# Attention values as plain float32 products, the two heads in the two column halves of the TensorE array

## The chip, the cores and the metric

The kernel runs on one core of a Trainium2 chip. Such a core has a matrix engine (TensorE, "PE" in the profile, with its weight loads as "PEld"), a vector engine (DVE), a scalar engine (ACT), a further vector engine that cannot reach the matrix engine's result banks (POOL), and queues that start transfers, here nearly all on SP. The matrix engine multiplies a loaded block of weights, up to 128 rows by 128 columns, with moving data of up to 512 columns, and adds into one of eight result banks, each of 128 partitions by 512 float32 values.

The metric is the device time of one launch in microseconds, the median of several runs. Lower is better.

## The reference

Eight batches of eight heads attend over 576 positions with heads of 64, masked by blocks of 64; then a feed-forward layer runs over all 4608 tokens. All inputs and the output are float32.

```python
def _attn_ref(q, k, v):                      # (8, 8, 576, 64) each
    scores = scale * np.matmul(q, k.transpose(0, 1, 3, 2))
    mask = block_i >= block_j                # blocks of 64 positions
    scores = np.where(mask, scores, -1000000000.0)
    scores = scores - np.max(scores, axis=-1, keepdims=True)
    attn = np.exp(scores)
    attn = attn / (np.sum(attn, axis=-1, keepdims=True) + 1e-09)
    return np.matmul(attn, v).astype(np.float32)

def _moe_ref(x, w_in, w_out, alpha):         # (4608, 512), (512, 2048), (2048, 512)
    h = x @ w_in
    g = np.maximum(h, 0.0) + alpha * np.minimum(h, 0.0)
    return (g @ w_out).astype(np.float32)
```

The last product of the attention, `attn @ v`, is called "the values" here.

## The kernel before

**Two ways to multiply.** A product in plain float32 is one call in the kernel. Most of the kernel does it another way: each operand is split into a high part, rounded to the type `float32r`, and a low part, the rest, and the sum of high x high, low x high and high x low is taken, each a product of the rounded type.

**Order of work.** The kernel does not issue its work as it is written. Every operation is handed to `Plan.op` with its engine, a cost, what it reads and writes, the buffers it takes, and a priority. `schedule` (L181) then plays the engines forward: whenever one is free it takes the ready operation of the lowest priority number, and the resulting order is the order of instructions in each queue. `SHIFTS` is a table that adds a small number to the priorities named in it. `Products` and the functions `c_...` give the costs that this planner counts with. `Buf` stands for a room in SBUF or a result bank that is handed out while planning. At most 6 of the 8 banks serve the attention at one time.

**Attention.** The 64 batch-heads go as 32 pairs of heads, pair `p` at priority `5 * p`. A pair has five query tiles (`query_tile`, L818): four of 128 queries of each head (j = 0 to 3) and one, j = 4, of the last 64 queries of both heads together. Each tile is scores on TensorE (L859; L854 for the early plain ones, L921 for j = 4), the maximum on DVE, the exponential on ACT (L875), the division by the sum on POOL (L883), transposes of the probabilities on TensorE (L891, L947, L956) and a copy of these out of the bank (`evac`, L961). The tiles are done in two parts: 4, 3, 2, and then 1, 0. For the first four pairs tiles 1 and 0 are done ahead of everything else.

**Values.** `values` (L976) runs after each part: for the span of queries 256 to 575 after tiles 4, 3, 2, and for 0 to 255 after tiles 1, 0. The key positions come in blocks of 128, and block c meets the queries from c * 128 on. So the later span has products of 320, 320, 320 and 192 columns and one of 64 columns for the last 64 keys, the earlier span one of 256 and one of 128. `NV = NP + 1 = 5` divides the pairs:

- Pairs 0 to 4 are plain. The transposed probabilities are copied once into `PTF` (one of two, in turn), the last block's into `P4F`. The weights are the 64 columns of V of one head, straight from where V was loaded (`vraw`). Each head's products go to partitions 0 to 63 of a bank (L994; L998 for the last 64 keys, which has 64 rows of weights), and ACT copies them to the head's half of `xT` (L1012).
- Pairs 5 to 31 are split. `evac` writes `PH` on ACT (L970) and `PL` on DVE (L971), of which there is one each. V is split into `V` on ACT and DVE (L764, L766). With the high part of the probabilities as moving data, the weights are V's high and low part side by side, 128 columns; with the low part, V's high part alone, 64 columns. For the last 64 keys both parts of the probabilities and V are stacked, `P4`. All are at L1004. The two halves of the bank are then added: ACT copies one to `tmp` (L1023) and DVE adds the other (L1025).

At pair 5 the rooms of the plain pairs (`pt0`, with `PTF` and the second room for V) are closed and those of the split pairs (`PH`, `PL`, `V`) opened.

**Feed-forward.** Chunks of 256 tokens run beside the attention for the first six of sixteen blocks of the hidden layer (`chunk_a`: L582 and L619), with low enough priorities to fill TensorE. The other ten blocks run after it, on chunks of 512 tokens (L660 and L619); their weights are prepared from about the end of the attention on (`later_weights`).

Of the kernel before, what the change touches and what calls it, by code (L numbers as in the profile page):

```python
# [9 lines left out]
F32 = mybir.dt.float32  # L10
# [10 lines left out]
NP = H // 2  # L21
NPAIR = B * NP
DM, DF, DO = H * D, 2048, 512
P = 128
# [15 lines left out]
WARM, WARM_END = 10, 3400  # L40
TICK, FULL_COLUMNS, SP0 = 3413.33, 3060, 700
LAG = 6.75
Q2B, TB = 1, 1
VP, VL, VE = 2.0, 1.0, 0.0
E0, E1 = -4.0, 1.0
NEAR, LP = 8.0, 1.0
FP = -1
XP = 2.0
AHEAD = {(8 + k // 2, k % 2): 12 + 4 * k for k in range(4)}
SHIFTS = {  # L50
    9: 2.6, 10: 1.7, 11: -0.8, 12: -0.5, 15: 2.4, 16: 2.1, 19: -5.7, 36: 3.1, 42: 1.1, 59: 0.6, 60: -0.7, 61: 1.4, 81.1574: 2.7, 99: -1,
    101.5278: -0.6, 119.5: 1.1, 121.8981: 0.2, 122.2685: 1.7, 153.5: 1.1, 154.5: 0.3, 155: -0.8, 155.5: 0.8, 156.5: -1.6, 175.2315: 1.4,
    180.4167: -1.6, 184.8611: -3.9,
}
SOON, XB = 150, 1006.7
FEW = 12
# [1 line left out]
B1 = 10  # L58
RB, EB = 2, 2
LO_A = ("POOL", "POOL")  # L60
NV = NP + 1
PB = 6
GB = 6
LAT = {"PE": 250, "DVE": 130, "ACT": 140, "POOL": 140}
# [205 lines left out]
def c_dve(n):  # L270
    return 65 + n / 0.96
# [6 lines left out]
def c_act(n, sbuf=False):  # L278
    return (93 if sbuf else 51) + n / 1.2
# [27 lines left out]
def c_mm(n, rows=P):  # L307
    return Products(max(n / 2.22, 107) + 2, max(n / 1.2, 213), n * rows / P)


def c_tr(light=False):
    return Products(109, 213, 256, 50.0, light)

# [8 lines left out]
def attn_ffn(ctx, tc, qT, kT, vT, w_in, w_out, alpha, out):  # L322
# [49 lines left out]
    def pt_key(p):  # L372
        return p % 2 if p < NV else 2

    def pt_of(p, i):

        if i == 2:
            return P4F[p % 2] if p < NV else P4
        return PTF[p % 2] if p < NV else pt[i]
# [22 lines left out]
    def rooms(pool, *kinds):  # L402
        for kind, n, shape, dt in kinds:
            plan.room(kind, n, lambda i, kind=kind, shape=shape, dt=dt: (pools[pool] if isinstance(pool, str) else pool).tile(
                [P, *shape], dt, name=f"{kind}{i}"))

    rooms(wraw, ("raw", RB, [1024], I32), ("m", EB, [512], F32))
    rooms(st, ("qraw", 1, [QP], F32), ("kraw", 1, [S], F32), ("vraw", 1, [5, 2, D], F32), ("p", PB, [512], F32), ("pl", 1, [S], F32), ("tmp", TB, [448], F32),
          ("nm", 4, [2], F32), ("nm2", 2, [2], F32), ("s", 4, [2, 2], F32), ("s3", 2, [3], F32), ("sp", 4, [2], F32), ("ri", 4, [2], F32))


# [562 lines left out]
    def values(p, v_parts, spans, pr):  # L974


        V, vkeys = v_parts
        b, pair = divmod(p, NP)
        r0 = (b * S) % RING
        shared = {q0: Buf("bank", "att") for q0, q1, _ in spans if q1 - q0 <= 256}  # L980
        for h in range(2):
            lo, hi = (slice(0, 64), slice(64, 128)) if h == 0 else (slice(64, 128), slice(0, 64))
            for q0, q1, part in spans:
                n = q1 - q0
                ob, tmp = shared.get(q0) or Buf("bank", "att"), Buf("tmp")
                at = h * n if q0 in shared else 0
                pkeys = [("PT", pt_key(p), h, j, x) for j in range(4) for x in range(2) if P * j < q1 and q0 < P * j + P]
                if q1 == S:
                    pkeys += [("PT", pt_key(p), h, j, x) for j in (4, 5) for x in range(2)]
                cs = [(c, max(q0, c * P)) for c in range(4) if c * P < q1]  # L990

                def plain(h=h, q0=q0, q1=q1, ob=ob, at=at, cs=cs):
                    for c, a in cs:
                        nc.tensor.matmul(ob()[0:64, at + a - q0:at + q1 - q0], V()[:, c, h, :],  # L994
                                         pt_of(p, 0)[:, h, 448 * c + a:448 * c + q1],
                                         start=(c == 0), stop=(c == cs[-1][0] and q1 < S))
                    if q1 == S:
                        nc.tensor.matmul(ob()[0:64, at + 512 - q0:at + S - q0], V()[0:64, 4, h, :], pt_of(p, 2)[0:64, h, :],  # L998
                                         start=False, stop=True)

                def mm(x, c, n, h=h, q0=q0, q1=q1, ob=ob, at=at, a=dict(cs)):

                    b = 512 if x == "x" else a[c]
                    nc.tensor.matmul(ob()[0:64 if x == "l" else P, at + b - q0:at + q1 - q0],  # L1004
                                     V()[:, c, 1 + h, :] if x == "l" else V()[:, c, 2 * h:2 * h + 2, :],
                                     P4[:, h, :] if x == "x" else pt[x == "l"][:, h, 448 * c + b:448 * c + q1],
                                     start=(n == 0), stop=(n < 0))
                if p < NV:
                    op("PE", sum(c_mm(4 * (q1 - a)) for _, a in cs) + (c_mm(256, 64) if q1 == S else 0), plain, r=vkeys + pkeys,
                       w=[(ob, h)], prio=pr)  # L1010
                    w = [("x", b % 2, pair, h, part)]
                    op("ACT", c_act(n), lambda ob=ob, at=at, n=n, q0=q0, hi=hi: nc.scalar.copy(  # L1012
                        out=xT[hi, pair, r0 + q0:r0 + q0 + n], in_=ob()[0:64, at:at + n]), r=[(ob, h)], w=w, prio=pr)
                    continue
                between = (("h", 1), ("h", 3), ("l", 3), ("x", 4), ("l", 0), ("l", 1), ("l", 2)) if q1 == S else (("l", 1), ("l", 0))
                for i, (x, c) in enumerate((("h", 0), *between, ("h", 2 if q1 == S else 1))):
                    last = i == len(between) + 1
                    n1 = 64 if x == "x" else q1 - dict(cs)[c]
                    op("PE", c_one(n1, x == "l"), lambda mm=mm, x=x, c=c, i=-1 if last else i: mm(x, c, i),
                       r=[*vkeys, *pkeys, *[(ob, h, "begun")] * (i > 0), *[(ob, h, k) for k in between if last], *[(ob, 0)] * (h and q0 in shared)],  # L1020
                       w=[(ob, h) if last else (ob, h, (x, c)) if i else (ob, h, "begun")], claim=[tmp] * (i == 0),
                       prio=pr + LP * (x == "l"))
                op("ACT", c_act(n) + HALF, lambda ob=ob, at=at, n=n, hi=hi, lo=lo, tmp=tmp: nc.scalar.copy(  # L1023
                    out=tmp()[hi, :n], in_=ob()[lo, at:at + n]), r=[(ob, h)], w=[tmp], prio=pr)
                op("DVE", c_dve(n) + (0 if h else HALF), lambda ob=ob, at=at, n=n, q0=q0, hi=hi, tmp=tmp: nc.vector.tensor_tensor(  # L1025
                    out=xT[hi, pair, r0 + q0:r0 + q0 + n], in0=ob()[hi, at:at + n], in1=tmp()[hi, :n], op=ALU.add),
                    r=[(ob, h), tmp], w=[("x", b % 2, pair, h, part)], prio=pr)

    def xs(b, parts=(0, 1)):
        return [("x", b % 2, pr, h, i) for pr in range(NP) for h in range(2) for i in parts]  # L1030
# [45 lines left out]
                done += CHA  # L1076

    def end_attention():
        att.close()
        pools["wb"] = ctx.enter_context(tc.tile_pool(name="wb", bufs=1, side="right"))  # L1080

# [92 lines left out]
```

## Time and profile before

| | |
|---|---|
| runs | 1126.52 us median of 3, from 1123.86 to 1128.25 |
| the profiled execution's own span | 1122.8 us |
| TensorE | 7288 products, busy 1106.1 us |
| DVE, ACT, POOL | busy 835.2, 715.3 and 613.4 us |
| values, split pairs (L1004) | 702 products, between 107.8 and 580.2 us |
| values, plain pairs (L994, L998) | 140 products, between 14.2 and 96.6 us |

Times in the views are microseconds from the start of the span, unless marked ns. In a row of a group stand the line, engine and operation, what is written and read, the shape of the weights (rows*columns) and of the moving data, the count, and then the busy time of the group and the mean duration of one in ns. Products are pipelined: the duration of one includes its way through the array, so the durations of a row of them overlap and add up to more than the time they take. What one costs is read from the pace, the time from one to the next. In the chain of waits each stretch begins where the one before it ends, so a stretch of n products there, divided by n, is the pace. The idle time of a group is followed by what ended it.

### The profile page before, as it was taken

What the parts mean: (1) busy time and instruction counts of PE and PEld (TensorE: products, weight loads), DVE (VectorE), ACT (ScalarE), POOL (GpSimd) and SP (SyncE); (2) the same over time, 40 slices, a digit from 0 to 9 for tenths busy, and PEclk for the clock granted to TensorE, in tenths of its full rate; (3) what the DMA queues carried; (4) which work ended last, traced back from release to release, by engine and by line L of the source; (5) the groups of instructions that cost most, each with busy time, mean ns of one, the idle gap of its engine ahead of it and who ended that gap; (6) DMA issues with size and microseconds to landing.
All of it is one profiled execution on the core that took longest, in us unless ns stands there. A gap on an engine that the chain in (4) does not pass through costs nothing.

```text
span 1122.8 us, 22035 instructions
## 1 busy us (share of the span) xinstructions
PE 1106.1 (99%) x7288; PEld 988.5 (88%) x7288; DVE 835.2 (74%) x1954; ACT 715.3 (64%) x1933; POOL 613.4 (55%) x769
## 2 busy tenths in 40 slices
PE   8999999999999999999999999999999999999998
PEld 5677989999999999999999888988988998998987
DVE  7888999888888888898857997564647465656554
ACT  7888988888888888788856655343434334343432
POOL 5767556656565556566549987243434334352422
PEclk9999999999999999999999999999999999999999
DMA  8797676576765576567324532221303030312021
GB/s 232 226 261 214 188 221 177 169 201 169 220 170 146 175 191 197 175 170 213 100 93 148 162 101 76 76 72 42 113 1 113 1 114 3 112 38 76 2 75 38
DMA packets 75314, 147.96 MB, mean 132 GB/s; under 512 B 9792, under 2 KB 11840, under 8 KB 75200
## 3 DMA queue, kind: packets, MB, share of 16 engines
q1 hardware_dynamic: 74768, 146.28, 44.4%
q8 instruction: 58, 0.95, 0.4%
q14 instruction: 56, 0.46, 0.1%
q10 hardware_dynamic: 432, 0.27, 0.1%
HBM read 68.40 MB, written 29.36 MB: 87 GB/s over the span
## 4 chain that ended last, share of the span: by engine, by line
PE 85%; DVE 7%; ACT 3%; POOL 2%; issue 2%; DMA 1%; SPq 0%; DVEq 0%; ACTq 0%; POOLq 0%
PE bank L619 33%; PE bank L660 19%; PE bank L582 11%; PE bank L1004 6%; PE bank L859 5%; PE bank L891 5%; PE bank L994 2%; PE bank L921 2%; PE bank L947 1%; ACT p L875 1%; DVE xh L568 1%; PE bank L854 1%; DVE PL L971 1%; DVE g L595 1%; POOL p L883 1%
## 5 line engine op out<-in xcount | busy, mean ns | idle before, releaser
L602 POOL TENSOR_TENSOR gl<-g,gh 128x256 fp32r<-128x256 f32 x288 | 220.0, 772 | 309.6 <-PE bank L660 173.5
L660 PEld LDWEIGHTS bank<-X,w 128*128 128x128 f32 x1890 | 253.7, 189 | 20.6 <-POOL X L488 1.2
L660 PE MATMUL bank<-X,w 128*128 128x256 f32 x1890 | 259.2, 281 | 0.6 <-POOL X L488 0.5
L619 PE MATMUL bank<-w,gh 128*128 128x512 f32 x720 | 225.7, 395 | 1.1 <-DVE g L669 0.7
L883 POOL TENSOR_SCALAR p<-p,ri 128x512 f32<-128x512 f32 (+3 forms) x256 | 153.0, 611 | 115.7 <-DVE ri L881 45.5
L593 ACT ACTIVATE g<-bank 128x256 f32<-128x256 f32 x288 | 110.7, 386 | 155.1 <-DVE bank L673 138.0
L599 ACT CAST gh<-g 128x256 fp32r<-128x256 f32 x288 | 117.0, 407 | 85.2 <-DVE g L595 84.0
L595 DVE SCALAR_TENSOR_TENSOR g<-g,oal,bank 128x256 f32<-128x256 f32 x288 | 136.0, 475 | 42.0 <-ACT g L593 36.6
L673 DVE TENSOR_TENSOR bank<-bank,g 128x256 f32<-128x256 f32 x180 | 76.1, 428 | 104.7 <-PE bank L660 103.2
L875 ACT ACTIVATE p<-bank,nm 128x512 f32<-128x512 f32 (+3 forms) x256 | 135.0, 532 | 20.9 <-DVE nm L872 6.9
L619 PE MATMUL bank<-w,gl 128*128 128x512 f32 x360 | 141.6, 393 | 0.0
L619 PE MATMUL bank<-wa,gh 128*128 128x512 f32 x432 | 140.0, 405 | 0.0
L619 PEld LDWEIGHTS bank<-w,gh 128*128 128x128 f32 x720 | 120.3, 188 | 14.2 <-DVE g L669 0.9
L582 PE MATMUL bank<-xh,wa 128*128 128x256 f32 x864 | 131.2, 287 | 0.4 <-DVE xh L568 0.4
L971 DVE TENSOR_TENSOR PL<-bank,PH 128x512 fp32r<-128x512 f32 (+2 forms) x189 | 111.8, 608 | 12.6 <-ACT PH L970 10.3
L582 PEld LDWEIGHTS bank<-xh,wa 128*128 128x128 f32 x864 | 114.8, 190 | 3.2 <-DVE xh L568 1.1
L891 PE MATMUL bank<-ident,p 128*128 128x128 f32 x640 | 109.4, 276 | 4.7 <-POOL p L883 3.2
L859 PE MATMUL bank<-K,Q 128*128 128x512 f32 (+1 forms) x472 | 104.2, 331 | 0.3 <-ACT p L875 0.2
L970 ACT CAST PH<-bank 128x512 fp32r<-128x512 f32 (+2 forms) x189 | 97.0, 529 | 11.0 <-PE bank L891 7.3
L669 DVE TENSOR_TENSOR g<-bank,g 128x256 f32<-128x256 f32 x135 | 56.8, 422 | 49.1 <-PE bank L660 47.8
L891 PEld LDWEIGHTS bank<-ident,p 128*128 128x128 f32 x640 | 75.3, 140 | 18.6 <-POOL p L883 8.3
L619 PE MATMUL bank<-wa,gl 128*128 128x512 f32 x216 | 85.5, 396 | 0.3 <-POOL gl L602 0.2
(124 smaller groups left out, 2016.7 us busy)
## 6 DMA issues: line engine op xcount, KB each, us to landing
Q<-QH SPq DMA_DIRECT2D x62, 256.0 KB, 3.8
K<-KH SPq DMA_DIRECT2D x124, 128.0 KB, 3.7
vraw<-in_v SPq DMA_DIRECT2D x32, 320.0 KB, 3.1
qraw<-in_q SPq DMA_DIRECT2D x31, 320.0 KB, 3.8
xd<-xT SPq DMA_DIRECT2D x8, 1152.0 KB, 5.7
part<-o SPq DMA_DIRECT2D x36, 256.0 KB, 3.2
xb<-xd SPq DMA_DIRECT2D x9, 1024.0 KB, 5.3
m<-part SPq DMA_DIRECT2D x36, 256.0 KB, 3.3
```

The source lines that it names most:

```text
L582: nc.tensor.matmul(hp()[:, :n], ww()[:, 0, cc * P:(cc + 1) * P], x()[:, cc, :n], start=(i == 0 and cc == 0), stop=(i == 2 and cc == NCC - 1))
L593: op("ACT", c_act(CHA), lambda: nc.scalar.activation(out=g(), in_=hp()[:, ts], func=AF.Relu, scale=-1.0), r=[hp], w=[g], prio=FP)
L595: op("DVE", c_dve(CHA) + 60, lambda: nc.vector.scalar_tensor_tensor(out=g(), in0=g(), scalar=oal[:, f:f + 1], in1=hp()[:, ts], op0=ALU.mul ...
L599: op("ACT", c_act(CHA, True), lambda: nc.scalar.copy(out=gh(), in_=g()), r=[g], w=[gh], prio=FP)
L602: op("POOL", c_pool(CHA), lambda: nc.gpsimd.tensor_tensor(out=gl(), in0=g(), in1=gh().bitcast(F32), op=ALU.subtract), r=[g, gh], w=[gl], p ...
L619: nc.tensor.matmul(acc(), a()[:, ts], ww(), start=(first and i == 0), stop=(last and i == 2))
L660: nc.tensor.matmul(bank()[:, :CHA], W()[:, i, 256 * at + P * c:256 * at + P * c + P], B()[:, j, CHA * c:CHA * c + CHA], start=(n == 0), st ...
L859: nc.tensor.matmul(o, Q()[:, i, qs], K()[:, 2 * h + i, :w], start=(i == 0), stop=(i == 1))
L875: op("ACT", 238 + w / 1.2, lambda h=h, t=t: nc.scalar.activation(out=t()[:, :w], in_=sb[h]()[:, off[h]:off[h] + w], func=AF.Exp, bias=nm() ...
L883: op("POOL", 244 + w / 1.2, lambda h=h: nc.gpsimd.tensor_scalar(out=pts[h]()[:, :w], in0=pts[h]()[:, :w], scalar1=ri()[:, h:h + 1], scalar ...
L891: nc.tensor.transpose(out=tp()[:, base + c * P:base + (c + 1) * P], in_=pts[h]()[:, c * P:(c + 1) * P], identity=ident)
L971: op("DVE", c_dve(n) + (HALF if n == P else 0), lambda: nc.vector.tensor_tensor(out=lo(), in0=src(), in1=hi().bitcast(F32), op=ALU.subtrac ...
```

## The change

`NV` becomes the number of pairs, so every pair goes the way of the plain ones; `PTF`, `P4F` and the two rooms for V stay open until the end of the attention, and `PH`, `PL`, `V` and `tmp` are not made any more. `values` is rewritten: one bank per span and pair, head 0 into partitions 64 to 127 and head 1 into 0 to 63. Each key block is one operation of the planner with the products of both heads, head 0 first. The first block begins the sums, the others follow, the last 64 keys ahead of the last product, which is that of block 1. One ACT copy over 128 partitions then moves the result of both heads to `xT`. `c_pair` is the cost that the planner counts for such an operation. `SHIFTS` is another table: 38 entries in place of 26. The branch for split pairs is still written in `values`, but no pair takes it.

```diff
--- before.py
+++ after.py
@@ -40,17 +40,19 @@
 WARM, WARM_END = 10, 3400
 TICK, FULL_COLUMNS, SP0 = 3413.33, 3060, 700
 LAG = 6.75
-Q2B, TB = 1, 1
+Q2B = 1
 VP, VL, VE = 2.0, 1.0, 0.0
 E0, E1 = -4.0, 1.0
 NEAR, LP = 8.0, 1.0
 FP = -1
 XP = 2.0
+PAIR = 20
 AHEAD = {(8 + k // 2, k % 2): 12 + 4 * k for k in range(4)}
 SHIFTS = {
-    9: 2.6, 10: 1.7, 11: -0.8, 12: -0.5, 15: 2.4, 16: 2.1, 19: -5.7, 36: 3.1, 42: 1.1, 59: 0.6, 60: -0.7, 61: 1.4, 81.1574: 2.7, 99: -1,
...
+    7: 2.7, 9: 3.8, 15: 4.6, 16: 2.1, 19: -11.3, 35.5: -2.3, 36: 3.1, 40.5: 2, 42: 5, 45.5: 1.3, 50: 4.1, 51.1574: -2.7, 51.5278: -2.5,
...
 }
 SOON, XB = 150, 1006.7
 FEW = 12
@@ -58,7 +60,7 @@
 B1 = 10
 RB, EB = 2, 2
 LO_A = ("POOL", "POOL")
-NV = NP + 1
+NV = NPAIR
 PB = 6
 GB = 6
 LAT = {"PE": 250, "DVE": 130, "ACT": 140, "POOL": 140}
@@ -308,6 +310,11 @@
     return Products(max(n / 2.22, 107) + 2, max(n / 1.2, 213), n * rows / P)
 
 
+def c_pair(n):
+
+    return Products(max(n / 2.4, 107) + PAIR, max(n / 1.2, 213) + PAIR, n)
+
+
 def c_tr(light=False):
     return Products(109, 213, 256, 50.0, light)
 
@@ -405,7 +412,7 @@
                 [P, *shape], dt, name=f"{kind}{i}"))
 
     rooms(wraw, ("raw", RB, [1024], I32), ("m", EB, [512], F32))
-    rooms(st, ("qraw", 1, [QP], F32), ("kraw", 1, [S], F32), ("vraw", 1, [5, 2, D], F32), ("p", PB, [512], F32), ("pl", 1, [S], F32), ("tmp", TB, [448], F32),
+    rooms(st, ("qraw", 1, [QP], F32), ("kraw", 1, [S], F32), ("vraw", 1, [5, 2, D], F32), ("p", PB, [512], F32), ("pl", 1, [S], F32),
           ("nm", 4, [2], F32), ("nm2", 2, [2], F32), ("s", 4, [2, 2], F32), ("s3", 2, [3], F32), ("sp", 4, [2], F32), ("ri", 4, [2], F32))
 
 
@@ -977,54 +984,46 @@
         V, vkeys = v_parts
         b, pair = divmod(p, NP)
         r0 = (b * S) % RING
-        shared = {q0: Buf("bank", "att") for q0, q1, _ in spans if q1 - q0 <= 256}
-        for h in range(2):
-            lo, hi = (slice(0, 64), slice(64, 128)) if h == 0 else (slice(64, 128), slice(0, 64))
-            for q0, q1, part in spans:
-                n = q1 - q0
-                ob, tmp = shared.get(q0) or Buf("bank", "att"), Buf("tmp")
-                at = h * n if q0 in shared else 0
-                pkeys = [("PT", pt_key(p), h, j, x) for j in range(4) for x in range(2) if P * j < q1 and q0 < P * j + P]
-                if q1 == S:
-                    pkeys += [("PT", pt_key(p), h, j, x) for j in (4, 5) for x in range(2)]
-                cs = [(c, max(q0, c * P)) for c in range(4) if c * P < q1]
-
-                def plain(h=h, q0=q0, q1=q1, ob=ob, at=at, cs=cs):
-                    for c, a in cs:
-                        nc.tensor.matmul(ob()[0:64, at + a - q0:at + q1 - q0], V()[:, c, h, :],
-                                         pt_of(p, 0)[:, h, 448 * c + a:448 * c + q1],
-                                         start=(c == 0), stop=(c == cs[-1][0] and q1 < S))
-                    if q1 == S:
-                        nc.tensor.matmul(ob()[0:64, at + 512 - q0:at + S - q0], V()[0:64, 4, h, :], pt_of(p, 2)[0:64, h, :],
-                                         start=False, stop=True)
-
-                def mm(x, c, n, h=h, q0=q0, q1=q1, ob=ob, at=at, a=dict(cs)):
-
-                    b = 512 if x == "x" else a[c]
-                    nc.tensor.matmul(ob()[0:64 if x == "l" else P, at + b - q0:at + q1 - q0],
-                                     V()[:, c, 1 + h, :] if x == "l" else V()[:, c, 2 * h:2 * h + 2, :],
-                                     P4[:, h, :] if x == "x" else pt[x == "l"][:, h, 448 * c + b:448 * c + q1],
-                                     start=(n == 0), stop=(n < 0))
-                if p < NV:
-                    op("PE", sum(c_mm(4 * (q1 - a)) for _, a in cs) + (c_mm(256, 64) if q1 == S else 0), plain, r=vkeys + pkeys,
-                       w=[(ob, h)], prio=pr)
-                    w = [("x", b % 2, pair, h, part)]
-                    op("ACT", c_act(n), lambda ob=ob, at=at, n=n, q0=q0, hi=hi: nc.scalar.copy(
-                        out=xT[hi, pair, r0 + q0:r0 + q0 + n], in_=ob()[0:64, at:at + n]), r=[(ob, h)], w=w, prio=pr)
-                    continue
-                between = (("h", 1), ("h", 3), ("l", 3), ("x", 4), ("l", 0), ("l", 1), ("l", 2)) if q1 == S else (("l", 1), ("l", 0))
-                for i, (x, c) in enumerate((("h", 0), *between, ("h", 2 if q1 == S else 1))):
-                    last = i == len(between) + 1
-                    n1 = 64 if x == "x" else q1 - dict(cs)[c]
-                    op("PE", c_one(n1, x == "l"), lambda mm=mm, x=x, c=c, i=-1 if last else i: mm(x, c, i),
-                       r=[*vkeys, *pkeys, *[(ob, h, "begun")] * (i > 0), *[(ob, h, k) for k in between if last], *[(ob, 0)] * (h and q0 in shared)],
-                       w=[(ob, h) if last else (ob, h, (x, c)) if i else (ob, h, "begun")], claim=[tmp] * (i == 0),
-                       prio=pr + LP * (x == "l"))
-                op("ACT", c_act(n) + HALF, lambda ob=ob, at=at, n=n, hi=hi, lo=lo, tmp=tmp: nc.scalar.copy(
-                    out=tmp()[hi, :n], in_=ob()[lo, at:at + n]), r=[(ob, h)], w=[tmp], prio=pr)
-                op("DVE", c_dve(n) + (0 if h else HALF), lambda ob=ob, at=at, n=n, q0=q0, hi=hi, tmp=tmp: nc.vector.tensor_tensor(
-                    out=xT[hi, pair, r0 + q0:r0 + q0 + n], in0=ob()[hi, at:at + n], in1=tmp()[hi, :n], op=ALU.add),
-                    r=[(ob, h), tmp], w=[("x", b % 2, pair, h, part)], prio=pr)
+        rows = slice(64, 128), slice(0, 64)
+        for q0, q1, part in spans:
+            n = q1 - q0
+            ob = Buf("bank", "att")
+            cs = [(c, max(q0, c * P)) for c in range(4) if c * P < q1]
+
+            def pkeys(c, xs, q0=q0, q1=q1):
+                if c > 3:
+                    return [("PT", pt_key(p), h, 5, x) for h in range(2) for x in xs]
+                js = [j for j in range(c, 4) if P * j < q1 and q0 < P * j + P] + [4] * (q1 == S)
+                return [("PT", pt_key(p), h, j, x) for h in range(2) for j in js for x in xs]
+
+            def mm(x, c, first, last, q0=q0, q1=q1, ob=ob, a=dict(cs)):
+
+                b = 512 if c > 3 else a[c]
+                at = slice(b - q0, q1 - q0)
+                for h in range(2):
+                    to = ob()[rows[h], at]
+                    if p < NV:
+                        k = slice(0, 64 if c > 3 else P)
+                        moving = pt_of(p, 2)[0:64, h, :] if c > 3 else pt_of(p, 0)[:, h, 448 * c + b:448 * c + q1]
+                        nc.tensor.matmul(to, V()[k, c, h, :], moving, start=first, stop=last)
+                        continue
+                    moving = P4[:, h, :] if c > 3 else pt[x == "l"][:, h, 448 * c + b:448 * c + q1]
+                    nc.tensor.matmul(to, V()[:, c, 3 * h if x == "v" else 1 + h, :], moving, start=first, stop=last)
+            if p < NV:
+                work = [("p", c) for c, _ in cs] + [("p", 4)] * (q1 == S)
+                work = work[:1] + work[2:] + work[1:2]
+            else:
+                cs4 = [c for c, _ in cs] + [4] * (q1 == S)
+                hs = [(x, c) for c in cs4 for x in "hv"]
+                work = hs[:1] + hs[2:] + [("l", c) for c in cs4 if c < 4] + hs[1:2]
+            for i, (x, c) in enumerate(work):
+                last = i == len(work) - 1
+                n1 = 64 if c > 3 else q1 - dict(cs)[c]
+                op("PE", c_pair(4 * n1 if x == "p" else n1), lambda mm=mm, x=x, c=c, i=i, last=last: mm(x, c, i == 0, last),
+                   r=[*vkeys, *pkeys(c, {"p": (0, 1), "l": (1,)}.get(x, (0,)) if c < 4 else (0, 1)), *[(ob, "begun")] * (i > 0), *[(ob, k) for k in work[1:-1] if last]],
+                   w=[ob if last else (ob, (x, c)) if i else (ob, "begun")], prio=pr + LP * (x == "l"))
+            op("ACT", c_act(n), lambda ob=ob, n=n, q0=q0: nc.scalar.copy(out=xT[:, pair, r0 + q0:r0 + q0 + n], in_=ob()[:, :n]),
+               r=[ob], w=[("x", b % 2, pair, h, part) for h in range(2)], prio=pr)
 
     def xs(b, parts=(0, 1)):
         return [("x", b % 2, pr, h, i) for pr in range(NP) for h in range(2) for i in parts]
@@ -1076,6 +1075,7 @@
                 done += CHA
 
     def end_attention():
+        pt0.close()
         att.close()
         pools["wb"] = ctx.enter_context(tc.tile_pool(name="wb", bufs=1, side="right"))
 
```

More of the change, by code (lines that the diff above doesn't have):

```diff
@@ L48 @@
 XP = 2.0
+PAIR = 20
 AHEAD = {(8 + k // 2, k % 2): 12 + 4 * k for k in range(4)}
 SHIFTS = {
-    9: 2.6, 10: 1.7, 11: -0.8, 12: -0.5, 15: 2.4, 16: 2.1, 19: -5.7, 36: 3.1, 42: 1.1, 59: 0.6, 60: -0.7, 61: 1.4, 81.1574: 2.7, 99: -1,
-    101.5278: -0.6, 119.5: 1.1, 121.8981: 0.2, 122.2685: 1.7, 153.5: 1.1, 154.5: 0.3, 155: -0.8, 155.5: 0.8, 156.5: -1.6, 175.2315: 1.4,
-    180.4167: -1.6, 184.8611: -3.9,
[4 rows of a table added]
 }
```

3 rows, old and new, of the table SHIFTS are left out of this document.

## The prediction

> **What bounds the kernel now.** I read the head of the page, then a table of busy time by stretch of the span (each engine's busy us with its instruction count, then the granted clock), then who TensorE (PE) waited for.
>
> ```profile
> PE 1106.1 (99%) x7288; PEld 988.5 (88%) x7288; DVE 835.2 (74%) x1954; ACT 715.3 (64%) x1933; POOL 613.4 (55%) x769
> ...
> PEclk9999999999999999999999999999999999999999
> ```
> ```profile
> 0.00:100.00 100.00, 91.35 (x512) 64.53 (x513) 80.84 (x208) 81.26 (x220) 64.53 (x89) 1.00 0.87 244
> 100.00:580.00 480.00, 477.86 (x3430) 443.59 (x3429) 413.92 (x1053) 403.06 (x1153) 283.03 (x386) 1.00 0.62 173
> 580.00:720.00 140.00, 137.82 (x865) 122.36 (x864) 112.26 (x206) 75.65 (x176) 111.79 (x116) 1.00 0.39 129
> 720.00:1100.00 380.00, 380.00 (x2384) 341.94 (x2383) 219.62 (x472) 150.56 (x374) 149.00 (x172) 1.00 0.17 56
> ```
> ```profile
> PE bank L891 <- POOL p L883: 3.2, 8, 0.8
> PE bank L994 <- ACT PTF L968: 1.8, 3, 1.1
> PE bank L854 <- DVE o L774: 1.5, 1, 1.5
> PE bank L1004 <- DVE PL L971: 1.2, 1, 1.2
> ```
>
> PE idles 8.65 us in the first 100 us, 2.1 in the next 480, 2.2 in the stage between the attention and the long last one, and not at all in that; its clock is full in every stretch. A busy PE need not be a PE at its peak, so I checked the pace on the chain of waits (start, length, what). The 512-column products are 6.29/27 = 0.233 us each, one column per 0.455 ns, with nothing between them:
>
> ```profile
> 583.38 6.29 PE bank L619 x27
> ```
>
> The other chain rows below run at the same kind of even pace. So this kernel is bound by PE work. Vector and scalar time matters only where PE waits for it, and that is a few us in all: no wait for DVE or ACT above sums to 2 us. **The change is therefore worth what it does to PE's time for the values.** What it saves on DVE and ACT is large, but covered by PE already.
>
> **The values before.** Rows of groups (mean ns of one at the end), then the chain for one head of a split pair and one of a plain pair.
>
> ```profile
> L1004 PE MATMUL bank<-PH,V 128*128 128x320 f32 x162 | 44.1, 322 | 1.2 <-DVE PL L971 1.2
> L994 PE MATMUL bank<-PTF,vraw 128*64 128x320 f32 x60 | 18.3, 441 | 0.2 <-ACT PTF L968 0.2
> L994 PEld LDWEIGHTS bank<-PTF,vraw 128*64 128x64 f32 x120 | 14.9, 136 | 14.2 <-ACT PTF L968 3.1 <-DVE PTF L966 0.4 <-ACT gh L599 0.3
> L998 PE MATMUL bank<-P4F,vraw 64*64 64x64 f32 x20 | 3.2, 242 | 0.0
> ```
> ```profile
> 108.11 1.11 PE bank L1004 x9
> ...
> 577.56 0.35 PE bank L1004 x4
> ```
> ```profile
> 65.92 2.08 PE bank L994 x8
> 68.00 0.25 PE bank L998 x2
> 68.25 2.08 PE bank L994 x8
> 70.34 0.26 PE bank L998 x2
> 70.59 0.48 PE bank L891 x3
> ```
> ```profile
> 91.83 1.08 PE bank L994 x4
> ...
> 95.41 1.46 PE bank L994 x8
> ...
> 573.60 0.22 PE bank L891 x2
> ```
>
> Split pairs (5 to 31, 27 of them): 162 = 27 pairs x 2 heads x 3 blocks, so a split product is one instruction. A head costs 1.11 us for the span of queries 256 to 575 (9 products) and 0.35 for queries 0 to 255 (4). A pair is 2 x 1.46 = 2.92 us, and 27 pairs 78.8 us.
>
> Plain pairs (0 to 4): 60 = 5 x 2 x 3 x 2, so a plain product is **two** instructions. Four of 320 columns take 1.08 us, 0.270 each, which is 0.84 ns a column; by columns that is 0.162 for 192, 0.216 for 256, 0.108 for 128 and 0.054 for 64.
>
> Now the important reading. Six of 320 and two of 192 should be 6 x 0.270 + 2 x 0.162 = 1.94, but the row says 2.08: **0.14 us too much**. Four of 256 and four of 128 should be 1.30, and are 1.46: 0.16. Two of 64 (the last key block, 64 rows by 64 columns) should be 0.11, and are 0.25: 0.14. Three transposes behind them should be 3 x 0.11 = 0.33, and are 0.48: 0.15. So every step between the shapes 128x128, 128x64 and 64x64 of plain products costs PE some 0.15 us, about the 136 ns of one weight load. The split products do not pay it although half of them are 64 columns wide too: the whole later span of a head takes 1.11, of which its columns alone, 1216 + 1152 at 0.455 ns, explain 1.08.
>
> The five plain pairs thus cost 5 x [2 x (2.08 + 0.25) + 1.46] = 30.6 us, and leaving their 10 spans for other work 10 x 0.15 = 1.5. **Values now: 78.8 + 32.1 = 110.9 us of PE.**
>
> **The change, part by part.** (1) All 32 pairs go plain, each product of head 0 and of head 1 in its own column half. If the halves overlap fully, a product of both heads costs what one head's two instructions cost: the later span 2 x (3 x 0.270 + 0.162 + 0.054) = 2.05, the earlier one 2 x (0.216 + 0.108) = 0.65, together 2.70 a pair and 86.4 us for 32. No row of before has two halves at work, so this is bounded: 86.4 with full overlap, 172.8 with none.
>
> (2) Steps between shapes. A span of a pair is at best one run, 64 runs in all (28 pairs with both spans after their last tile, four whose earlier span comes first). Each is entered and left: 64 x (0.14 + 0.15) = 18.6 us. In the 32 later spans the 64-row block comes ahead of the last product, so there and back is 32 x (0.14 + 0.15) = 9.3. Sum **27.9 us**, where the present plain pairs pay about 5, which is in their 32.1 already. Below, a run could pay half of it, if the idle half loads its weights meanwhile. Above, each run that other work cuts in two adds 0.29; today's values are cut, as here by transposes:
>
> ```profile
> 313.33 0.29 PE bank L1004 x2
> 313.62 0.11 PE bank L891
> 313.73 0.23 PE bank L1004 x2
> ```
>
> If half of the new runs were cut once, that would be 32 x 0.29, some 9 us.
>
> (3) How the halves overlap. Program order is: head 0's two instructions, then head 1's two. The second of head 0 needs the first to be through; if PE begins its products in order, head 1 starts one instruction late. In a long row the two then run evenly beside each other, but at the end of every row (a change of shape) the last instruction of head 1 runs alone. The rows end on lengths 192, 64, 320 in the later span and 128 in the earlier: 0.162 + 0.054 + 0.270 + 0.108 = 0.59 us a pair, **19.0 us** over 32. Where lengths change inside a row (320 to 192, 256 to 128) another 0.11 each would be lost, 6.9 us at most. The lower end is 0. I take 19.0, since every chain row above shows one product after another and none shows two begun together.
>
> The Trainium skill bears on just this. "TensorE: Matmul & The Clock Gate", Part 3, What overlaps and what doesn't, says "MATMULs are pc-monotone in start AND end", which gives the 19.0; "TensorEngine Tiling (Array Packing)", Key Properties, says that tiles work independently, and the former page gives a few ns for each further tile, which gives 0. No run here shows either yet.
>
> (4) DVE and ACT lose the split: PL (L971), V's two parts (L764, L766), the copy to tmp and the add (L1023, L1025). Three of their rows, from the page and the groups, and V's load from the page's list of transfers (KB each, us to landing):
>
> ```profile
> L971 DVE TENSOR_TENSOR PL<-bank,PH 128x512 fp32r<-128x512 f32 (+2 forms) x189 | 111.8, 608 | 12.6 <-ACT PH L970 10.3
> ...
> L1025 DVE TENSOR_TENSOR xT<-bank,tmp 64x320 f32<-64x320 f32 x54 | 26.3, 487 | 7.5 <-ACT tmp L1023 6.5
> L1023 ACT COPY tmp<-bank 64x320 f32<-64x320 f32 x54 | 22.7, 421 | 10.3 <-PE bank L1004 7.6 <-issue 1.2
> ...
> vraw<-in_v SPq DMA_DIRECT2D x32, 320.0 KB, 3.1
> ```
>
> The two vector rows alone are 138 us off DVE's 835, worth nothing while PE is full. A part may come back: PE's idle time of the first 100 us (8.65). But there the cheaper plain values also leave PE less to do, and the waits quoted above, on POOL's p and ACT's PTF, are left in. I take 0, with -5 and +5 as ends. The probabilities' home doubles and V is read from where it was loaded, two buffers in turn; V's load has two pairs' time, 2 x 17.8 (480/27) us, so SP's queue and the Q and K moves behind it are not held up.
>
> (5) The new priorities move work about. With PE full they can gain only part of the same idle time, and can lose as much: 0, inside the same ends.
>
> **The sum:** values after = 86.4 + 27.9 + 19.0 = 133.3; before 110.9; +22.4 us on a profiled span of 1122.8. The runs' median, 1126.52, is 3.7 above that span; the difference is added to the median: **1149 us**.
>
> **The rivals.**
> *A, the halves start together.* Then (3) is 0 and values are 114.3: +3.4, **1130 us**, with the ends of (4) 1125 to 1135. For it: nothing in the kernel ties head 1 to head 0. Against: the one-by-one rows.
> *B, faster: the step between shapes is hidden.* Its place is the start of each run; its price is the 27.9 us of (2). The 0.15 us are about one weight load (136 ns) standing bare; with two halves the second may load while the first starts. With the halves together and half of the steps paid, values are 86.4 + 14 = 100.4: -10.5, and up to 5 us of idle time back, **1113 us** (1106 to 1119). It decides once a pair costs under 110.9/32 = 3.47 us of PE, against 4.17 in my sum. Against it: L998, whose weights are loaded the same way, pays 0.14 each time.
> *C, the change does not do what it says: no overlap.* 172.8 + 27.9 = 200.7: +90, **1216 us**. Against it: different halves and different outputs, no shared place that the program shows.
>
> **How the numbers follow.** Forecast (with 6.9 more for uneven lengths, 9 for cut runs, and down to 10 if the halves overlap in part: 1136 to 1162) 0.45; A 0.25; B 0.22; C 0.08. The range reaches from the middle of B to the top of the forecast, 1110 to 1162; it leaves out C and a half of B's tail, under 0.2. Within 0.5% (5.6 us, about what a measurement of this kernel can tell from no change) is most of A, 0.18; faster is B and a little of A, 0.26; slower is the forecast, C and a little of A, 0.56.
>
> **What would show it.** In the changed trace: plain products twice per block and head, 64 columns each. Overlap shows as a chain in which a block's four instructions of 320 columns pass in 0.54 us (1.08: C). Order shows in starts: head 1's first together with head 0's second (forecast) or with its first (A). The steps show as rows that are 0.14 us over their columns' time, 192 of them or more (B: half or none). PE should stay at 98 to 99%, DVE fall to about 60%. The prediction is wrong if the values' PE time is near 100 us, or if PE is no longer full: then the order of work, which I set at nothing, decides.

## The result and the profile after

The changed kernel took **1134.83 us**, median of 4 runs (1131.06 to 1135.86), against 1125.19 for the kernel before (4 runs, 1123.23 to 1128.25): a ratio of 1.0078, with a 95% interval of 1.0060 to 1.0097. It is slower by 9.6 us. The forecast was 1149, slower by 22.4: the way was right and the size was more than double.

The profiled execution of the changed kernel has a span of 1129.3 us. The head of its page, and its table of busy time by stretch (busy us with counts for PE, PEld, DVE, ACT, POOL, then the granted clock, the transfer engines' busy share and GB/s):

```profile
PE 1113.1 (99%) x7342; PEld 944.3 (84%) x7342; DVE 666.7 (59%) x1603; ACT 654.1 (58%) x1788; POOL 600.0 (53%) x769
```
```profile
0.00:100.00 100.00, 89.09 (x572) 65.11 (x573) 83.44 (x218) 80.45 (x222) 68.55 (x96) 0.98 0.90 258
100.00:580.00 480.00, 479.98 (x3370) 392.31 (x3370) 245.43 (x690) 339.36 (x998) 264.18 (x376) 1.00 0.61 169
580.00:720.00 140.00, 138.57 (x876) 123.03 (x877) 106.95 (x200) 77.44 (x179) 112.25 (x117) 1.00 0.40 131
```

DVE lost 168.5 us and ACT 61.2, and PE is as full as ever: after the first 100 us it idles 1.45 us up to 720, where it idled 4.3 before. In the first 100 us it idles more, 10.9 us against 8.65, and its clock is no longer whole there.

The chain of waits around the values of a pair (start, length, what), first the later span, then the earlier span of another pair, and last, as a measure, four feed-forward products (L589) with no values beside them:

```profile
265.93 0.44 PE bank L898 x4
266.37 2.50 PE bank L1008 x20
268.87 0.66 PE bank L589 x4
```
```profile
411.96 0.80 PE bank L1008 x8
412.76 1.15 PE bank L866 x6
...
419.61 0.48 PE bank L589 x4
```

Twenty products take 2.50 us. One after another their columns alone would be 12 x 0.270 + 4 x 0.162 + 4 x 0.054 = 4.10; half of it is 2.05. So **the two halves overlap fully** (the twenty start in ten pairs, 6 to 7 ns apart), and 0.45 us is left, three steps between shapes of 0.15 (in, to the 64 rows, back). The eight of the earlier span take 0.80: half of their columns' time is 0.65, and one step is 0.15. Leaving costs 0.66 - 0.48 = 0.18. A pair is 2.50 + 0.80 + 2 x 0.18 = 3.66 us and 32 pairs 117.1. Counted in the order of the trace, the values stand in 72 runs, 8 more than there are spans, each worth up to 0.15 + 0.18: 2.6. **Values after: 119.7 us of PE, against 110.9 by the same kind of rows before: +8.8 us**, about the measured loss.

That agreement is partly luck. I also counted both traces from the start of each product to the start of the next, and took off the usual pace of the other products beside the values. By that count, good to about 2 us, the values take some 121 us after and 116 before: the split pairs took about 83 us, 4 more than the 78.8 that their rows gave. The two profiled executions are 6.5 us apart, less than the medians, because that of the changed kernel was the fastest of its four runs.

### The profile page after: what moved, and what is told of

Same layout as the page of the kernel before. It is cut to its first block, busy times and chain, and to the rows that moved or that the text cites. A ratio compares the mean times of both kernels' runs of the same rounds, so it can differ in the third digit from the quotient of the medians.

```text
span 1129.3 us, 21572 instructions
## 1 busy us (share of the span) xinstructions
PE 1113.1 (99%) x7342; PEld 944.3 (84%) x7342; DVE 666.7 (59%) x1603; ACT 654.1 (58%) x1788; POOL 600.0 (53%) x769
## 4 chain that ended last, share of the span: by engine, by line
PE 93%; DVE 2%; POOL 2%; DMA 1%; ACT 1%; issue 1%; SPq 0%; POOLq 0%; ACTq 0%; DVEq 0%
PE bank L626 35%; PE bank L667 19%; PE bank L589 13%; PE bank L1008 9%; PE bank L866 6%; PE bank L898 6%; PE bank L928 2%; PE bank L954 1%; DMA Q<-QL 1%; PE bank L861 1%; DMA kraw<-in_k 0%; ACT p L882 0%; POOL X L495 0%; DMA qraw<-in_q 0%; POOL gl L609 0%
## 5 line engine op out<-in xcount | busy, mean ns | idle before, releaser
L890 POOL TENSOR_SCALAR p<-p,ri 128x384 f32<-128x384 f32 (+3 forms) x256 | 138.2, 554 | 110.5 <-DVE ri L888 48.9
L882 ACT ACTIVATE p<-bank,nm 128x128 f32<-128x128 f32 (+3 forms) x256 | 134.5, 532 | 28.6 <-DVE nm L873 14.7
L589 PE MATMUL bank<-xh,wa 128*128 128x256 f32 x864 | 130.6, 288 | 1.9 <-POOL wa L495 1.5
L589 PEld LDWEIGHTS bank<-xh,wa 128*128 128x128 f32 x864 | 115.0, 190 | 10.3 <-issue 2.7
L975 ACT COPY PTF<-bank 128x512 f32<-128x512 f32 (+2 forms) x192 | 94.9, 520 | 27.5 <-PE bank L898 25.6
L898 PE MATMUL bank<-ident,p 128*128 128x128 f32 x640 | 102.1, 278 | 5.0 <-POOL p L890 3.4
L1008 PE MATMUL bank<-PTF,vraw 128*64 128x320 f32 (+3 forms) x768 | 106.4, 393 | 0.3 <-ACT PTF L975 0.3
L898 PEld LDWEIGHTS bank<-ident,p 128*128 128x128 f32 x640 | 74.7, 141 | 23.8 <-POOL p L890 11.2
L879 DVE TENSOR_REDUCE nm<-bank 128x1 f32<-128x512 f32 (+1 forms) x128 | 76.3, 617 | 26.9 <-PE bank L866 26.3
```

The costliest lines, as they stand in the source:

```text
L589: nc.tensor.matmul(hp()[:, :n], ww()[:, 0, cc * P:(cc + 1) * P], x()[:, cc, :n], start=(i == 0 and cc == 0), stop=(i == 2 and cc == NCC - 1))
L882: op("ACT", 238 + w / 1.2, lambda h=h, t=t: nc.scalar.activation(out=t()[:, :w], in_=sb[h]()[:, off[h]:off[h] + w], func=AF.Exp, bias=nm() ...
L890: op("POOL", 244 + w / 1.2, lambda h=h: nc.gpsimd.tensor_scalar(out=pts[h]()[:, :w], in0=pts[h]()[:, :w], scalar1=ri()[:, h:h + 1], scalar ...
L898: nc.tensor.transpose(out=tp()[:, base + c * P:base + (c + 1) * P], in_=pts[h]()[:, c * P:(c + 1) * P], identity=ident)
L1008: nc.tensor.matmul(to, V()[k, c, h, :], moving, start=first, stop=last)
```

## The experiments

Each ratio is to the kernel before, run in turn on the same chip, with its 95% interval. The experiments ran on three chips, on which the median of the kernel before was 1125.08 to 1126.06 us, so differences of a microsecond between two experiments say little. Unless it says otherwise, a kernel starts from the changed one.

### Steps between shapes: 128 rows for the last key block

```diff
-    P4F = [pool0.tile([64, 2, 64], F32, name=f"P4F{i}") for i in range(2)]
+    P4F = [pool0.tile([P, 2, 64], F32, name=f"P4F{i}") for i in range(2)]
+    for i in range(2):
+        nc.gpsimd.memset(P4F[i][64:128], 0.0)
...
-                        k = slice(0, 64 if c > 3 else P)
-                        moving = pt_of(p, 2)[0:64, h, :] if c > 3 else ...
+                        k = slice(0, P)
+                        moving = pt_of(p, 2)[:, h, :] if c > 3 else ...
```

V's fifth block holds the last 64 positions twice, so the rows of weights below are there, and they meet zeros.

> The last key block of 64 gets 128 rows (the probabilities' rows 64 to 127 are zeros), so the later span keeps the shape 128x64 from its first to its last product; the columns are the same. Theory S (the loss of the changed kernel is in the steps between shapes): each of its long runs, 2.50 us on the chain of the changed kernel, loses two of three steps and becomes some 2.2 us; 32 x 0.29 = 9 us less than the changed kernel, so about 1126, level with the kernel before. Rival P (the new order of work costs the time, the steps are hidden by other work): within 3 us of the changed kernel.

Measured: 1125.35 us, ratio 1.0000 (0.9989 to 1.0010), 9.5 us less than the changed kernel by the medians and 8.8 by the ratios. The chain of this kernel has the same twenty products at

```profile
265.60 2.21 PE bank L1010 x20
```

0.29 us less than 2.50, times 32 is 9.3. In both traces the runs of values stand in the same places among the same other products, so the order of work can't be the cause. The steps are real, are worth 0.145 us each, and nothing hides them. One shape of 64 rows in 32 places cost what the whole change lost.

### Steps between shapes: fewer runs

```diff
-            values(p, v_parts, [span], pr + k + .5)
+            if p < NP:
+                values(p, v_parts, [span], pr + k + .5)
+        if p >= NP:
+            values(p, v_parts, [span for _, span in HALVES], pr + k + .5)
```

> For pairs 4 to 31 both spans of values are issued together after the pair's last tile: some 28 of the changed kernel's 72 runs of values go, each with one step in (0.15) and one out (0.15 to 0.20). Theory S: 28 x 0.33 = 9 us less than the changed kernel, some 1126. Rival P: no gain, or a loss of several us, as the later span's values come later than the order was tuned for.

Measured: 1133.51 us, ratio 1.0065 (1.0052 to 1.0079): 1.3 us less, within the intervals. The edit did not do what I meant. The values come together, but each key block is an operation of its own, and the planner puts others between, as the chain of this kernel shows:

```profile
313.95 1.55 PE bank L1008 x12
315.50 0.26 PE bank L898
315.77 0.95 PE bank L1008 x8
316.72 0.26 PE bank L898
```

One transpose (0.11 where nothing is around it) cuts a span in two, and takes 0.26 itself. In the order of the trace the runs are 73, not 44. The run says nothing against the steps.

So the next version makes the values of a pair (from pair 4 on) a single operation of the planner, on top of the 128 rows:

```diff
+            todo.append((q0, q1, part, n, ob, cs, pkeys, mm, work))
+        def all_of(todo):
+            for q0, q1, part, n, ob, cs, pkeys, mm, work in todo:
+                for i, (x, c) in enumerate(work):
+                    mm(x, c, i == 0, i == len(work) - 1)
...
+        op("PE", cost, lambda: all_of(todo), r=[*vkeys, *dict.fromkeys(k for t in todo for _, c in t[8] for k in t[6](c, (0, 1)))],
+           w=[t[4] for t in todo], prio=pr)
```

> 128 rows for the last key block as in e1_rows128, and for pairs 4 to 31 both spans' values as one operation of the planner after the last tile, so that no other work can come between: 36 runs in place of 72. Theory S: e1_rows128 less 36 x 0.33 = 12 us, about 1114 (down to 1116 for a later start of the values). Rival P (order): no gain over e1_rows128, 1125.

Measured: **1119.23 us**, ratio 0.9939 (0.9922 to 0.9955), faster than both kernels. A pair's 28 products are one run on its chain:

```profile
304.99 2.86 PE bank L1011 x28
```

2.70 of columns and one step. The values, 28 x (2.86 + 0.18) and four pairs in two runs each, should be 98.6 us now, 21 less than in the changed kernel; the time fell by 15.6. The expectation of 1114 was 5 too low. The first 100 us do not explain that: PE idles 13.35 us there (first row), but 13.94 in e1_rows128 (second row), from which the expectation was counted. From 100 to 720 us PE idles 2.0 us more than in e1_rows128; where the other 3 went is not shown.

```profile
0.00:100.00 100.00, 86.65 (x569) 65.41 (x570) 84.47 (x222) 81.47 (x226) 70.73 (x100) 0.98 0.93 256
0.00:100.00 100.00, 86.06 (x553) 63.73 (x554) 82.22 (x215) 78.62 (x218) 67.19 (x95) 0.98 0.88 250
```

### How the halves overlap

The prediction charged 19.0 us for head 1 starting one instruction behind head 0. The chain above has none of it. Two kernels look at why; both make a span one operation of the planner, so that their orders of work are the same (in the traces too). The control keeps the heads in turn within a key block; the other issues all of head 0's products of a span, then all of head 1's:

```diff
             def all_of(work=work, mm=mm):
-                for i, (x, c) in enumerate(work):
-                    for h in range(2):
+                for h in range(2):
+                    for i, (x, c) in enumerate(work):
                         mm(x, c, i == 0, i == len(work) - 1, h)
```

> A span's values are one operation of the planner, head 0 and head 1 in turn within each key block as in the changed kernel. Control for the next run. Runs of values should fall from 72 to 64, at most 3 us less than the changed kernel by theory S.

> As the control, but in each span all of head 0's products are issued ahead of all of head 1's. Theory I (products start in the order of the program, and the halves overlap only where neighbours in the program differ in their half): hardly any overlap, values take some 86 us more of TensorE than in the control, 1215 or so. Theory Q (each half takes its own next product from what is queued): no difference from the control, under 5 us.

Measured: the control 1133.28 us, ratio 1.0061 (1.0046 to 1.0077), 1.5 less than the changed kernel; heads one behind the other 1186.23 in a single run, 53 us more than the control. That is neither of the two theories. The chain of the control (first) and of the other (second), with a later and an earlier span each:

```profile
309.68 2.50 PE bank L1006 x20
...
317.79 0.80 PE bank L1006 x8
```
```profile
314.39 4.29 PE bank L1006 x20
...
323.59 0.81 PE bank L1006 x8
```

In the **earlier** span four products of head 0 stand ahead of the first of head 1, and still all eight take 0.81 us, against 0.80 in the control, and start in four pairs, 13 ns apart: TensorE took head 1's products past those that waited for head 0's half. In the **later** span little overlaps, and (4.29 - 2.50) x 32 is 57 us, about the measured 53. The order of its products in time, columns and count (timeline of the same kernel):

```profile
314.31 1.62 PE L1006 MATMUL bank<-PTF,vraw 128*64 128x320 f32 x6
315.86 0.33 PE L1006 MATMUL bank<-P4F,vraw 64*64 64x64 f32 x2
316.12 1.62 PE L1006 MATMUL bank<-PTF,vraw 128*64 128x320 f32 x8
317.67 0.32 PE L1006 MATMUL bank<-P4F,vraw 64*64 64x64 f32 x2
317.92 0.75 PE L1006 MATMUL bank<-PTF,vraw 128*64 128x320 f32 x2
```

Six of head 0 run alone; in the program, head 1's first stand behind head 0's two products of 64 rows. Only the eight in the middle, head 0's last two and head 1's first six, fit in the time of six. So nothing was taken past a step to another shape. Whether it is the step that stops it, or the distance (ten products rather than four), these runs do not tell apart.

### The early and the late pairs, each alone

Two kernels have the changed values in only a part of the pairs: the kernel before with them in pairs 0 to 4, and the changed kernel with the old plain values there.

```diff
+    def values(p, v_parts, spans, pr):
+        (values_new if p < NV else values_old)(p, v_parts, spans, pr)
```
```diff
+    def values(p, v_parts, spans, pr):
+        (values_new if p > NP else values_old)(p, v_parts, spans, pr)
```

> The kernel before, with the changed kernel's values (both heads at once, one bank, one copy) in pairs 0 to 4 alone; pairs 5 to 31 stay split, the old priorities stay. TensorE has some 14 us less to do in the first 100 us (32.6 us of values become 5 x 3.65). Theory E (in the first 100 us the transfers set the pace, so that time saved on TensorE there becomes idle time): within 3 us of the kernel before. Rival F (TensorE's work counts the same everywhere): 13 us less, about 1113.

> The changed kernel, with the old plain values (a head at a time, copies of 64 partitions) in pairs 0 to 4; its priorities stay. Theory E: the 14 us more of TensorE's work fit in where it idles and loses clock in the first 100 us: at most 7 us above the changed kernel. Rival F: 14 us above it, about 1148.

Measured: early alone **1122.88 us, ratio 0.9973** (0.9957 to 0.9989), 3.2 less than before; late alone **1142.50, ratio 1.0146** (1.0128 to 1.0164), 16.4 more than before and 7.7 more than the changed kernel. By rows the early pairs save 32.1 - 5 x 3.66 = 13.8 us of PE. They gave 3.2 in the one kernel and 7.7 in the other, just outside what theory E allowed and far from the 13 and 14 of rival F. The table of the first kernel, and the chain of the changed kernel in that stage, show where a part of the rest goes:

```profile
0.00:100.00 100.00, 86.65 (x531) 61.08 (x532) 81.88 (x214) 78.14 (x215) 65.65 (x91) 0.97 0.90 253
```
```profile
61.71 6.30 DMA Q<-QL
...
68.03 3.81 DMA qraw<-in_q
...
81.86 5.35 DMA kraw<-in_k
```

In the first kernel PE's idle time in the first 100 us goes from 8.65 to 13.35 us, 4.7 of the 10.6 us that did not arrive. The granted clock there goes from 1.00 to 0.97: it stood at half for two windows of 3.4 us, which can cost 1.7 us each. Its twelve runs show the same: the two with a mean clock of 1.000 took 1119.54 and 1119.92 us, the one with 0.993 took 1127.66. The rest is not accounted for. Between 20 and 100 us, plain values on PE have the largest share of the chain of the kernel before (32.0%); in the changed kernel the loads and moves of Q and K above have 19.4% of it. The transfer engines are 0.90 busy there, and were 0.87 before. That these transfers set the pace, and that PE had no other work ready, is argued, not shown.

The late pairs cost 16.4 us. By rows it is 27 x (3.66 - 2.92) = 20.0, and more with cut runs. Most of the missing 4 to 6 us was in the old split values, which took about 83 us by the count from start to start and not 78.8. Why they did is argued, not shown: from 100 us on they stand in 160 separate runs, and I had read their price from two heads that nothing cut.

### The load of DVE

```diff
+            if flat and p > NP:
+                op("DVE", c_dve(n), lambda: nc.vector.tensor_tensor(out=junk[:, :n], in0=flat(), in1=junk[:, :n], op=ALU.subtract),
+                   r=[*rk, *w], prio=pr)
```

> The changed kernel, with a subtraction on DVE behind each copy of probabilities of pairs 5 to 31, of the same size and from the same bank as the low parts (PL) had, into a scratch tile: 189 of them, some 110 us more of DVE. Theory S (TensorE is full, so what DVE was spared bought nothing): within 3 us of the changed kernel. Rival D (the freed DVE and the earlier freed banks gave some of the loss back): 5 us or more above it.

Measured: 1137.34 us, ratio 1.0098 (1.0082 to 1.0114); with the changed kernel at 1.0078 (1.0060 to 1.0097) that is 2.5 us more, and the intervals overlap. From 100 to 580 us DVE is busy 345.12 us in place of 245.43, and PE 479.63 in place of 479.98:

```profile
100.00:580.00 480.00, 479.63 (x3359) 391.53 (x3357) 345.12 (x871) 338.02 (x992) 267.32 (x376) 1.00 0.60 172
```

A hundred us of vector work were worth 2.5 us; the intervals allow anything from nothing to about 5, so rival D is not quite excluded. So what the change took off DVE was worth a few us at most, as far as this load stands for it (100 us put back of 168.5).

### The priorities

The changed kernel with the old table:

> The changed kernel with the table of priorities of the kernel before. My prediction set the new table at nothing, within 5 us either way. Theory S says the same: TensorE's work is equal, and only its idle time in the first 100 us can move: within 5 us of the changed kernel. Rival P (the new table was made for the new costs and carries some of the result): 5 to 15 us above the changed kernel.

Measured: 1146.94 us, ratio 1.0182 (1.0163 to 1.0200), **11.7 us more** than with the new table. My "within 5 us" falls. Its table of stretches:

```profile
0.00:100.00 100.00, 85.37 (x523) 59.45 (x523) 80.64 (x212) 77.16 (x211) 62.77 (x89) 0.98 0.89 250
100.00:580.00 480.00, 477.98 (x3325) 388.12 (x3326) 247.58 (x681) 335.38 (x983) 267.43 (x375) 1.00 0.61 170
580.00:720.00 140.00, 137.40 (x871) 119.81 (x870) 104.28 (x192) 80.25 (x190) 112.37 (x119) 1.00 0.36 118
```

Against the changed kernel PE idles 3.7 us more in the first 100 us, 2.0 in the next 480 and 1.2 up to 720; the runs of values are 80, not 72 (8 x 0.33 = 2.6). That is 9.5 us of the 15.9 between the two profiled executions (1145.2 and 1129.3; the medians are 11.7 apart). The rest is not accounted for.

### The loads of the first weights

The last question was what the first 100 us wait for. Both kernels start from the faster version above (1119.23) and change the spacing of the first six blocks of weights, `C0, C1 = 3.0, 4.0`, to 6.0 and to 3.0.

> f2_rows_pair_run with the loads of the first six blocks of weights at wider priorities (6 in place of 4 a block), so that in the first 100 us fewer of them stand ahead of the pairs' Q and K. Theory E (the transfers of that stage set the pace, and Q and K are what the pairs wait for): up to 4 us less than f2_rows_pair_run, 1115. Rival W (TensorE waits there for these weights): some us more.

> The same the other way, 3 in place of 4 a block. Theory E: up to 4 us more than f2_rows_pair_run. Rival W: some us less, since the feed-forward products that could fill TensorE come sooner.

Measured: later 1124.62, ratio 0.9991 (0.9982 to 1.0000); earlier 1126.58, ratio 1.0010 (1.0002 to 1.0019). **Both are slower** than the 0.9939 in between. Theory E fits the second and not the first, theory W the first and not the second. The first 100 us of the two (later, then earlier):

```profile
0.00:100.00 100.00, 87.47 (x551) 63.49 (x552) 82.34 (x217) 80.29 (x223) 64.42 (x95) 0.98 0.91 257
0.00:100.00 100.00, 82.78 (x511) 60.87 (x512) 81.42 (x205) 74.78 (x203) 62.70 (x89) 0.93 0.89 253
```

With the later loads PE idles 12.5 us there, less than the 13.35 of the faster version, and the kernel is slower all the same; with the earlier ones it idles 17.2, at a lower clock. New priorities move other work too, so these runs do not say what that stage waits for. It stays open.

## Why the prediction was right and wrong

**PE bounds the kernel, and vector time is covered: right.** 168 us less on DVE and 61 on ACT came with a slower kernel, and 100 us put back on DVE moved it by 2.5, within the intervals.

**Full overlap costs 86.4 us of PE: right.** 2.05 and 0.65 us a pair are on the chain.

**Values before, 110.9 us: too low by about 5.** The price of a split pair came from heads that nothing cut, though the prediction itself shows split values cut by transposes. From start to start the split pairs took about 83 us and not 78.8, the plain ones about 33 and not 32.1.

**Steps between shapes, 27.9 us: right in kind, a little small; rival B, which hid a half of them, falls.** Inside the runs they are 0.15 each as read from the kernel before; leaving costs 0.18 rather than 0.15, and 8 runs were cut: 0.96 us a pair (3.66 - 2.70) is 30.7 us, and 2.6 for the cuts, which I had only in the upper end. Taking 64 of them away gave 9.5 us. The count of 64 runs was right, although both spans do not come after a pair's last tile: the later span is issued after tiles 4, 3, 2.

**The order of the halves, 19.0 us: wrong, it is 0.** This is the step that failed, and rival A had it. I took PE to begin its products in the order of the program, on the strength of rows in which one product follows another. But in those rows neighbouring products all needed the same half. A row in which nothing could have overlapped says nothing about what would. The Trainium skill supported the wrong side here: "TensorE: Matmul & The Clock Gate", Part 3, What overlaps and what doesn't, has products starting in strict program order. With the heads one behind the other, the eight products of an earlier span took 0.81 us; in strict order head 1's first could begin beside head 0's fourth at best, and they would need 0.54 + 0.65 = 1.19 and a step. The measurement decides: between column halves the order is not strict, though no run shows it past a step to another shape.

**Savings in the first 100 us, priced like any other: wrong.** The sum took 13.8 us of the early pairs' values at full worth and bounded what could get lost there at 5. The early pairs returned 3.2 us alone, and 7.7 in the changed kernel.

**The new priorities, 0 within 5: wrong, they are worth 11.7.** They keep PE filled and the runs whole. I read PE's small idle time of the kernel before as all that an order could win, but that idle time goes with a table that fits the costs: with other costs under it, the old table leaves 6.9 us more up to 720 us.

**Luck.** Rival A's sum, the forecast without the 19.0, is 1130, within 5 us of the result. It has the late pairs at +17.6 us and the early ones at -14.2; they measured +16.4 and -7.7. The late pairs come out right because two errors went against each other: steps that cost some 5 us more than in the sum, and split values that had cost some 4 us more. The miss is in the early pairs. With the old table the kernel was 11.7 us slower still, and rival A would have been that much further off.

## What to carry to other kernels

Before using a part of the array, count the changes of shape that come with it, and read their price where the kernel already has one: here 0.15 us going in and 0.18 coming out; 192 such steps ate the whole gain of the two halves. Then keep such products in one shape and in one run; padding 64 rows to 128 with zeros took no time that shows and gave 9.5 us, and whole runs took the kernel to 0.9939 of the time before. And a microsecond saved on the bounding engine need not be worth one: 13.8 saved in the first 100 us gave 3.2 in one kernel and 7.7 in another.

## What the hardware showed that I had not expected

- TensorE took the other half's products past four waiting ones: heads in turn and heads one behind the other gave 0.80 and 0.81 us for eight products of 128x64, whose columns in two halves at once are worth 0.65. No run shows it past a step to another shape.
- A transpose that cuts a run of half-width products takes longer too: 0.26 us in place of 0.11.
- The granted clock goes with how full single windows are, not with the sum of the gaps. In these traces it is full or half, in windows of 3.41 us. The first 100 us had 10.9 us of idle time in the changed kernel and 11.2 in the control of the halves, and mean clocks of 0.98 and 0.95. In the twelve other kernels, every stretch at half clock between 20 and 110 us came right behind a window in which PE was busy 33 to 57%. Two more windows as empty (53 and 57%) had none behind them, and neither had any fuller window. Why that is so is not shown. In the changed kernel, with PE busy 1.59 us of 3.41, and then the clock at 0.50:

```profile
61.53:64.94 3.41, 1.59 (x12) 1.18 (x10) 3.41 (x10) 2.44 (x8) 2.07 (x3) 1.00 0.96 235
64.94:68.35 3.41, 3.03 (x13) 2.60 (x14) 3.41 (x7) 2.36 (x6) 2.19 (x4) 0.50 1.05 250
```
